# Agent attention with a gated convolution: query weights laid out in overlapping groups of four columns, 22 agents copied from rows four apart, and one buffer of transposed rows per batch

## The chip, the core and the metric

The kernel runs on one core of a Trainium2 chip. The metric is device time in microseconds (us), the median of several executions. The core has five engines with a queue each: PE (matmuls; its weight loads are shown as PEld), DVE (vector), ACT (scalar), POOL (GpSimd) and SP, which here only issues DMA transfers. A queue is worked off in order: an instruction that waits holds up all that stand behind it. Engines wait for each other through semaphores.

## The reference, cut to what matters

```
B, N, C = 4, 12800, 128          # 49 agents per batch
def sm(a, b):                    # softmax over the last axis
    s = (a @ b.T) / sqrt(C);  e = exp(s - max(s));  return e / (sum(e) + 1e-9)
agent_v = sm(agents, k) @ v      # 49 x 128 per batch
x       = sm(q, agents) @ agent_v            # N x 128
gate    = sigmoid(sum_k conv_w[k] * x[n - 4 + k])   # 5 taps, causal, zeros ahead of a batch
out     = (gate * (x @ w_val)) @ w_out
```

All inputs and the output are float32.

## The kernel before, in words

**Folding.** x itself is never made. Since x = W agent_v, with W the 49 softmax weights of each query, the five taps of the gate and the value projection are linear in W. For each batch `fold_weights` (lines 513 to 730) multiplies agent_v by the five tap weights and by w_val, so that the gate and the value of a query come straight from its weights W and those of the four queries ahead of it. The main loop is then matmuls over rows of W (one row an agent, one column a query).

**Three products for one.** The matmuls run in float16, and a float32 number is held as a high and a low part. For each agent three products are needed: high weight by high matrix, low weight by high matrix, high weight by low matrix. That is 147 rows; a matmul takes 128. The 128 rows of `pt` (lines 777 to 798) are 49 low parts (POOL, L794), 49 high parts (ACT, L779) and 30 of the high parts again (POOL, L784). The high parts of the 19 agents that are left lie in a second tile, `x2`, each five times, shifted by one query from tap to tap: 95 rows, so that one matmul serves all taps (L926 for the gate, L953 for the value). The matrices beside them, `wst`, are built row by row to match (lines 570 to 631) and transposed on PE (L659) into `stat`.

**Units, pairs, chunks.** A unit is 1280 queries (10 units a batch, 40 in all). `queries` (lines 733 to 798): scores on PE (L376), transposed by DVE (L386), maximum (L745), subtraction on POOL (L750), exp on ACT (L758), sums (L763 to L767) and scaling (L772) on DVE, then the three steps that fill `pt`. `transposes` (line 827) turns `pt` into rows of W: on PE for the first four units (L849), by a DMA transpose from SP's queue for the other 36 (L835). Two units make a pair (20 in all, 5 a batch), which has a buffer of 2560 columns, one of a ring of four tiles `x1s`. The last four columns of the pair before are needed ahead of a pair's first column: `halo` (lines 813 to 825) copies them on POOL (L819), or writes zeros (L816) at the head of a batch. `shifts` (lines 866 to 891) then issues two DMA copies from x1 into x2 (L884), 15 agents and 4 agents. `gates`, `values` and `project` (lines 898 to 1025) work on chunks of 512 queries, 25 a batch: five tap matmuls (L922) and the x2 matmul (L926) for the gate, tanh on ACT (L935); two matmuls for the value (L949, L953); their product h on DVE (L962), its high part hh on ACT (L968), its low part hl on POOL (L973); three matmuls for the output (L992 to L994), scaled on ACT (L1006), and stored from SP (L1021).

**Keys and values.** Each batch also has ten units of keys (L376 again, copied by ACT at L402, maximum at L411) and ten of values (exp at L471, transposed at L386, matmuls at L480). Units of q, k and v are loaded by SP (L369) into a ring of 11 buffers.

**What sets the order.** PE's order is written out by hand (`order`, lines 1088 to 1114). The orders of ACT, DVE, POOL and SP come from a list scheduler (`Plan`, lines 68 to 173): each step carries an engine, an estimated cost in us, what it reads and writes and, for a transfer, the time on the wire; of the steps that are ready the one with the longest tail of work behind it goes first. When the estimates change, or steps fall away, the order of these four queues may change everywhere.

Of the kernel before, what the change touches and what calls it, by code (L numbers as in the profile page):

```python
# [32 lines left out]
THREES = 15  # L33
NDUP = 2 * THREES
X2R = 19
X2CUTS = ((0, THREES, 3, 0.5), (THREES, X2R, 1, 0.3))

# [4 lines left out]
NX = 4  # L42
# [134 lines left out]
def tile_agent_attention_gated_conv(  # L177
# [39 lines left out]
    qw = ring(NPT, [P, NBLK, A], F32, "qw")  # L217
# [3 lines left out]
    x1s = ring(NX, [P, PAD + SEG], F16, "x1_")  # L221
# [39 lines left out]
    tiny = const.tile([P, NBLK], F32, name="tiny")  # L261
    nc.scalar.dma_start(out=ag_sb, in_=agT)
# [6 lines left out]
    nc.vector.memset(x1s[0][:, 0:PAD], 0.0)  # L269
    for t in wst_sb:  # L270
        nc.gpsimd.memset(t[:, TAPS + 1 :, :], 0.0)
# [232 lines left out]
    avT = const.tile([P, A], F32, name="avT")  # L504
    mx = const.tile([P, 2], F32, name="mx")
    gw = const.tile([P, TAPS, A], F32, name="gw")
    gs = const.tile([P, TAPS, A], F32, name="gs")
# [5 lines left out]
    def fold_weights(b):  # L513
# [19 lines left out]
        def normalise():  # L533
            dve.tensor_scalar_add(den, pt[:, 0:A], 1e-9)
            dve.reciprocal(out=den, in_=den)
            dve.tensor_tensor(out=avT, in0=pt[:, AP_ : AP_ + A], in1=den, op=ALU.mult)
# [5 lines left out]
                out=gw, in0=avT.unsqueeze(1).to_broadcast([P, TAPS, A]),  # L542
                in1=conv_sb.unsqueeze(2).to_broadcast([P, TAPS, A]), op=ALU.mult,
# [4 lines left out]
        def gate_scale():  # L548
# [16 lines left out]
                out=pv[:, 0:A], lhsT=wval_sb, rhs=avT, start=True, stop=True  # L565
# [4 lines left out]
        x2g = wst[:, TAPS + 1, 0 : TAPS * X2R].rearrange("p (r k) -> p k r", k=TAPS)  # L570
        x2v = wst[:, TAPS + 2, 0 : TAPS * X2R].rearrange("p (r k) -> p k r", k=TAPS)
        ghi = wst[:, 0:TAPS, 0:A]
        vhi = wst[:, TAPS, 0:A]

        def threes(x):

            if len(x.shape) == 2:
                return x[:, 0 : 3 * THREES].rearrange("p (i r) -> p i r", r=3)
            return x[:, :, 0 : 3 * THREES].rearrange("p k (i r) -> p k i r", r=3)

        def rest(out, full, s, hi):
            dve.scalar_tensor_tensor(
                out=out, in0=full, scalar=rs[:, s : s + 1], in1=hi,
                op0=ALU.mult, op1=ALU.subtract,
            )

        def val_weights():
# [9 lines left out]
            dve.tensor_scalar_mul(vhi, pv[:, 0:A], rs[:, 1:2])  # L597
# [8 lines left out]
        def gate_weights():  # L606
            dve.tensor_scalar_mul(ghi, gw, rs[:, 0:1])
# [579 lines left out]
```

## Time and profile before

| | |
|---|---|
| three runs | 425.52, 428.47, 429.88 us; median 428.47 |
| profiled execution, first to last instruction (span) | 423.6 us |
| profiled execution, its own time | not on record beside its span |
| PE, DVE, ACT, POOL busy | 403.9, 293.3, 301.5, 228.2 us |
| mean granted clock of PE | 0.985 |
| moved by DMA | 127.62 MB, 301 GB/s on average |

How to read it: busy time is the time in which an engine had at least one instruction under way; loads of weights (PEld) overlap matmuls. A wait is put down to what ended last ahead of it. In a table of stretches, each engine's busy us stand in order PE, PEld, DVE, ACT, POOL, followed by the granted clock of PE, the DMA engines' mean busy share (packets overlap, so that it can pass 1) and GB/s. In a timeline, each row has start, duration, engine, line, operation, written tile and read tiles, and in brackets the idle time ahead of it with its releaser; "x" stands for x1, x1s and x2 alike, since buffer numbers are left out.

### The profile page before, as it was taken

To read this page: it belongs to the slowest core of one execution; us is meant where nothing else is said; L and a number is where in the kernel's file an instruction comes from. 1 tells how busy PE (TensorE), PEld (TensorE's weight loads), DVE (VectorE), ACT (ScalarE), POOL (GpSimd) and SP (SyncE) were. 2 spreads that over 40 slices of the span, in tenths; PEclk is the share of its full clock that TensorE was granted. 3 is DMA by queue.
4 is the path that set the end of the run, shared out by engine and by line. 5 is a ranking of instruction groups with operands and counts; after the bars stand their busy time and mean duration, and the time that the engine had idled before them with its cause. 6 is when DMAs were issued, how large, how long until landed. Compare 5 with 4: busy or idle time off the path is not lost.

```text
span 423.6 us, 10042 instructions
## 1 busy us (share of the span) xinstructions
PE 403.9 (95%) x3907; PEld 197.0 (47%) x3907; DVE 293.3 (69%) x562; ACT 301.5 (71%) x521; POOL 228.2 (54%) x263
## 2 busy tenths in 40 slices
PE   4979999999999999999999899999999989999995
PEld 1358434346555443446555343335555534344443
DVE  3757899867875978667795575767765678676231
ACT  1564568779966777678876486778876567788776
POOL 1002557654657565554566355574366277877553
PEclk9969999999999999999999899999999999999998
DMA  8999999999999999999999999999999977755733
GB/s 320 420 417 411 370 367 353 301 295 310 412 293 283 346 317 362 304 278 356 351 379 324 271 299 370 314 332 302 296 393 322 239 196 161 199 163 176 205 121 124
DMA packets 75129, 127.62 MB, mean 301 GB/s; under 512 B 50466, under 2 KB 50850, under 8 KB 75084
## 3 DMA queue, kind: packets, MB, share of 16 engines
q1 hardware_dynamic: 74940, 126.87, 96.9%
q8 instruction: 30, 0.49, 0.5%
q10 hardware_dynamic: 144, 0.13, 0.2%
q14 instruction: 15, 0.12, 0.1%
HBM read 79.25 MB, written 26.21 MB: 249 GB/s over the span
## 4 chain that ended last, share of the span: by engine, by line
PE 78%; DMA 9%; DVE 8%; ACT 1%; POOL 1%; issue 1%; SPq 0%; POOLq 0%; DVEq 0%; ACTq 0%
PE gate L922 23%; PE sc L376 17%; PE av L480 10%; PE val L949 5%; PE out L992 5%; PE val L953 5%; PE gate L926 5%; PE out L993 4%; DMA ld<-kT 4%; PE out L994 4%; DMA x<-pt 3%; DMA x<-x 2%; DVE h L962 1%; DVE qw L772 1%; DVE qsm L763 1%
## 5 line engine op out<-in xcount | busy, mean ns | idle before, releaser
L973 POOL TENSOR_TENSOR hl<-h,hh 128x512 f16<-128x512 f32 (+1 forms) x101 | 116.9, 1158 | 96.1 <-ACT hh L968 96.0
L922 PE MATMUL gate<-x,stat 128*128 128x512 f16 (+1 forms) x500 | 125.2, 380 | 0.2 <-ACT th L935 0.2
L962 DVE SCALAR_TENSOR_TENSOR h<-th,val 128x512 f32<-128x512 f32 x100 | 67.8, 678 | 66.8 <-PE out L993 26.2
L376 PE MATMUL sc<-ld,ag_sb 128*32 128x320 f32 x1280 | 101.5, 447 | 7.6 <-DMA ld<-kT 7.0
L935 ACT ACTIVATE th<-gate,unscale 128x512 f32<-128x512 f32 x100 | 68.3, 683 | 33.3 <-PE gate L926 31.7
L1006 ACT ACTIVATE ob<-out,oscale 128x512 f32<-128x512 f32 x98 | 67.3, 687 | 21.3 <-PE out L994 20.1
L922 PEld LDWEIGHTS <-stat 128*128 128x128 f16 x505 | 46.3, 97 | 63.7 <-issue 14.8
L968 ACT CAST hh<-h 128x512 f16<-128x512 f32 (+1 forms) x101 | 61.5, 609 | 17.2 <-DVE h L962 16.4
L750 POOL TENSOR_TENSOR qw<-sT,qmx 128x490 f32<-128x490 f32 x40 | 41.4, 1035 | 47.6 <-DVE qmx L745 47.5
L376 PEld LDWEIGHTS sc<-ld,ag_sb 128*32 128x32 f32 x1280 | 36.7, 111 | 59.4 <-issue 25.7
L480 PE MATMUL av<-ld,eT 128*32 128x129 f32 (+1 forms) x1400 | 50.7, 279 | 1.0 <-DVE eT L386 1.0
L480 PEld LDWEIGHTS av<-ld,eT 128*32 128x32 f32 (+1 forms) x1400 | 47.1, 117 | 7.5 <-issue 2.5
L794 POOL TENSOR_TENSOR pt<-qw,pt 128x490 f16<-128x490 f32 x40 | 44.8, 1120 | 3.1 <-ACT pt L779 2.9
L471 ACT ACTIVATE e<-ks,kbias 128x320 f32<-128x320 f32 x80 | 39.3, 554 | 5.4 <-DVE eT L386 3.3
L386 DVE STREAM_TRANSPOSE sT<-sc 128x640 f32<-128x640 f32 x40 | 33.6, 839 | 13.4 <-PE sc L376 12.7
L402 ACT COPY ks<-sc 128x640 f32<-128x640 f32 x40 | 27.7, 691 | 21.2 <-PE sc L376 19.1
L386 DVE STREAM_TRANSPOSE eT<-e 128x640 f32<-128x640 f32 x40 | 33.5, 842 | 9.8 <-ACT e L471 5.2
L926 PE MATMUL gate<-x,stat 95*128 95x512 f16 x100 | 38.3, 383 | 1.5 <-DMA x<-x 1.5
L949 PE MATMUL val<-x,stat 128*128 128x512 f16 x100 | 38.2, 382 | 0.8 <-DVE h L962 0.6
L953 PE MATMUL val<-x,stat 95*128 95x512 f16 x100 | 38.1, 381 | 0.0
L994 PE MATMUL out<-hl,wo 128*128 128x512 f16 x98 | 37.0, 378 | 1.1 <-POOL hl L973 1.1
L992 PE MATMUL out<-hh,wo 128*128 128x512 f16 x98 | 37.3, 381 | 0.1
(130 smaller groups left out, 389.4 us busy)
## 6 DMA issues: line engine op xcount, KB each, us to landing
ld<-kT SPq DMA_DIRECT2D x40, 640.0 KB
ld<-qT SPq DMA_DIRECT2D x40, 640.0 KB
ld<-vP SPq DMA_DIRECT2D x39, 645.0 KB
outT<-ob SPq DMA_DIRECT2D x48, 512.0 KB
x<-x SPq DMA_DIRECT2D x18, 375.0 KB
x<-x SPq DMA_DIRECT2D x18, 100.0 KB
outT<-ob SPq DMA_DIRECT2D x3, 256.0 KB
x<-x SPq DMA_DIRECT2D x4, 187.5 KB
```

What stands on the lines that cost most here:

```text
L376: nc.tensor.matmul(out=out[g * BLK : (g + 1) * BLK, j, 0:GT], lhsT=ag_sb[:, b, j * BLK : (j + 1) * BLK], rhs=src[:, g * GT : (g + 1) * GT] ...
L386: nc.vector.transpose(out=out.rearrange("p n (j i) -> p j n i", j=2), in_=in_.rearrange("p j (n i) -> p j n i", i=BLK),)
L480: nc.tensor.matmul(out=av[o + j : o + j + cols, 0 : C + 1], lhsT=et[:, n, j : j + cols], rhs=vt[:, n, :], start=(u == 0 and n < 2), stop=( ...
L922: nc.tensor.matmul(out=pg, lhsT=stat[:, k, :], rhs=x1[:, c : c + w], start=(k == 0), stop=False,)
L926: nc.tensor.matmul(out=pg, lhsT=stat[0 : TAPS * X2R, TAPS + 1, :], rhs=x2[0 : TAPS * X2R, o2 : o2 + w], start=False, stop=True,)
L935: lambda: nc.scalar.activation(out=th, in_=pg, func=AF.Tanh, scale=unscale[:, 0:1]),
L949: nc.tensor.matmul(out=pv, lhsT=stat[:, TAPS, :], rhs=x1s[(b * NCH + n0 // CH) // 5 % NX][:, PAD + o2 : PAD + o2 + w], start=True, stop=False,
L953: nc.tensor.matmul(out=pv, lhsT=stat[0 : TAPS * X2R, TAPS + 2, :], rhs=x2[0 : TAPS * X2R, o2 : o2 + w], start=False, stop=True,)
L962: lambda: nc.vector.scalar_tensor_tensor(out=h, in0=th, scalar=1.0, in1=pv, op0=ALU.add, op1=ALU.mult),
L968: "act", 0.16 + 0.42 * scale, lambda: nc.scalar.copy(out=hh, in_=h),
L973: lambda: nc.gpsimd.tensor_tensor(out=hl, in0=h, in1=hh, op=ALU.subtract),
L1006: lambda: nc.scalar.activation(out=ob[:, o : o + w], in_=po, func=AF.Copy, scale=oscale),
```

## The change

- **Layout of `pt`** (rows of W). Rows 32 to 99 now hold 17 groups of four: group i holds the high parts of agents 3i-1 to 3i+2, so that every third agent stands there twice. `qw` is 52 columns wide, with a zero column ahead of the 49 and two behind them, and is read in groups of four that start every three columns. ACT writes 680 elements a block row in place of 490. Low parts lie in rows 98 to 127 and 0 to 20 (two POOL subtractions, 300 and 210 elements, in place of one of 490); 11 more duplicates lie in rows 21 to 31 (110 elements in place of 300).
- **x2** holds 22 agents in place of 19: 16 from rows 34, 38, ..., 94 and 6 from rows 77, 81, ..., 97, in partitions 16 to 125. Its matmuls take all 128 partitions, of which the others are zero.
- **x1** is one tile with five pairs of a batch side by side behind 16 zero columns, in place of a ring of four. The columns ahead of a pair are the tail of the pair before it, so `halo` is gone.
- **Weights.** `wst` follows the new layout: the high parts are written into the groups, ACT copies the high parts into the rows that meet low weights in two steps (`lows`) in place of one, and there are four remainders (`rests`) for gate and value. `gw`, `gs` and `avT` are 51 wide; `gs` borrows an output buffer.
- **Setup.** POOL clears `wst` as a whole, the three x2 tiles and the four qw tiles.
- Estimates for the planner: ACT 0.58 to 0.75 us, POOL 0.44 to 0.3 and 1.09 to 1.3, x2 copies 0.5 + 0.3 to 0.5 + 0.2 a unit.

The diff, cut to its core:

```diff
@@ -30,16 +30,34 @@
...
-THREES = 15
-NDUP = 2 * THREES
-X2R = 19
-X2CUTS = ((0, THREES, 3, 0.5), (THREES, X2R, 1, 0.3))
+AW = 52
+HI = 32
+FOURS = 17
+LOWS = ((HI + 4 * FOURS - 2, 0, 10), (0, 10, FOURS - 10))
+TWICE = 11
+AGAIN = HI - TWICE
+X2R = 22
+X2O = 16
+X2CUTS = ((0, 16, HI + 2, 0.5), (16, X2R, HI + 1 + 4 * TWICE, 0.2))
+def fours(x):
+    return x[:, :, HI : HI + 4 * FOURS].rearrange("p n (i r) -> p n i r", r=4)
+def threes(x, first, n, width):
+    ap = [tuple(d) for d in x.ap]
+    return bass.AP(x.tensor, x.offset + first, ap[:2] + [(3, n), (1, width)])
...
-NX = 4
+NX = 5
@@ -214,11 +232,11 @@
...
-    qw = ring(NPT, [P, NBLK, A], F32, "qw")
+    qw = ring(NPT, [P, NBLK, AW], F32, "qw")
...
-    x1s = ring(NX, [P, PAD + SEG], F16, "x1_")
+    x1 = const.tile([P, PAD + NX * SEG], F16, name="x1")
@@ -259,6 +277,7 @@
...
+    avT = const.tile([P, AW - 1], F32, name="avT")
@@ -266,9 +285,12 @@
...
-    nc.vector.memset(x1s[0][:, 0:PAD], 0.0)
+    nc.vector.memset(avT, 0.0)
+    nc.vector.memset(x1[:, 0:PAD], 0.0)
...
-        nc.gpsimd.memset(t[:, TAPS + 1 :, :], 0.0)
+        nc.gpsimd.memset(t, 0.0)
+    for t in x2s + qw:
+        nc.gpsimd.memset(t, 0.0)
@@ -501,10 +523,9 @@
...
-    avT = const.tile([P, A], F32, name="avT")
...
-    gw = const.tile([P, TAPS, A], F32, name="gw")
-    gs = const.tile([P, TAPS, A], F32, name="gs")
+    gw = const.tile([P, TAPS, AW - 1], F32, name="gw")
+    gs = obs[3][:, 0 : TAPS * (AW - 1)].rearrange("p (k a) -> p k a", k=TAPS)
@@ -533,14 +554,14 @@
         def normalise():
...
-            dve.tensor_tensor(out=avT, in0=pt[:, AP_ : AP_ + A], in1=den, op=ALU.mult)
+            dve.tensor_tensor(out=avT[:, 0:A], in0=pt[:, AP_ : AP_ + A], in1=den, op=ALU.mult)
         add("dve", 0.8, normalise, [at_t], ["avT"])
         add(
...
-                out=gw, in0=avT.unsqueeze(1).to_broadcast([P, TAPS, A]),
-                in1=conv_sb.unsqueeze(2).to_broadcast([P, TAPS, A]), op=ALU.mult,
+                out=gw, in0=avT.unsqueeze(1).to_broadcast([P, TAPS, AW - 1]),
+                in1=conv_sb.unsqueeze(2).to_broadcast([P, TAPS, AW - 1]), op=ALU.mult,
@@ -562,27 +583,43 @@
         add(
...
-                out=pv[:, 0:A], lhsT=wval_sb, rhs=avT, start=True, stop=True
+                out=pv[:, 0 : AW - 1], lhsT=wval_sb, rhs=avT, start=True, stop=True
...
-        x2g = wst[:, TAPS + 1, 0 : TAPS * X2R].rearrange("p (r k) -> p k r", k=TAPS)
-        x2v = wst[:, TAPS + 2, 0 : TAPS * X2R].rearrange("p (r k) -> p k r", k=TAPS)
-        ghi = wst[:, 0:TAPS, 0:A]
-        vhi = wst[:, TAPS, 0:A]
-        def threes(x):
-            if len(x.shape) == 2:
-                return x[:, 0 : 3 * THREES].rearrange("p (i r) -> p i r", r=3)
-            return x[:, :, 0 : 3 * THREES].rearrange("p k (i r) -> p k i r", r=3)
-        def rest(out, full, s, hi):
-            dve.scalar_tensor_tensor(
-                out=out, in0=full, scalar=rs[:, s : s + 1], in1=hi,
-                op0=ALU.mult, op1=ALU.subtract,
-            )
+        x2g = wst[:, TAPS + 1, X2O : X2O + TAPS * X2R].rearrange("p (r k) -> p k r", k=TAPS)
+        x2v = wst[:, TAPS + 2, X2O : X2O + TAPS * X2R].rearrange("p (r k) -> p k r", k=TAPS)
+        x2v = x2v[:, HALO : HALO + 1, :]
+        wg, wv = wst[:, 0:TAPS, :], wst[:, TAPS : TAPS + 1, :]
+        ghi, vhi = fours(wg), fours(wv)
+        pv3 = pv[:, 0 : AW - 1].unsqueeze(1)
+        def rests(full, hi, out, x2_, less):
+            n = X2R - 16
+            less(out[:, :, HI + 4 : HI + 4 * FOURS : 4], full[:, :, 2:A:3], hi[:, :, 0:16, 3])
+            less(out[:, :, AGAIN:HI], full[:, :, 0 : 3 * TWICE : 3], hi[:, :, 0:TWICE, 1])
+            less(x2_[:, :, 0:16], full[:, :, 1:A:3], hi[:, :, 0:16, 2])
+            less(x2_[:, :, 16:], full[:, :, 3 * TWICE : A : 3], hi[:, :, TWICE : TWICE + n, 1])
+        def lows(out, hi):
+            for to, i0, n in LOWS[::-1]:
+                nc.scalar.copy(
+                    out=out[:, :, to : to + 3 * n].rearrange("p k (i r) -> p k i r", r=3),
+                    in_=hi[:, :, i0 : i0 + n, 1:4],
+                )
+        def rest(s):
+            def less(out, full, hi):
+                dve.scalar_tensor_tensor(
+                    out=out, in0=full, scalar=rs[:, s : s + 1], in1=hi,
+                    op0=ALU.mult, op1=ALU.subtract,
+                )
+            return less
         def val_weights():
@@ -594,17 +631,11 @@
...
-            dve.tensor_scalar_mul(vhi, pv[:, 0:A], rs[:, 1:2])
-            pv3, hi3 = threes(pv[:, 0:A]), threes(vhi)
-            rest(
-                wst[:, TAPS, 2 * A :].rearrange("p (i r) -> p i r", r=2),
-                pv3[:, :, 0:2], 1, hi3[:, :, 0:2],
-            )
-            rest(x2v[:, HALO, 0:THREES], pv3[:, :, 2], 1, hi3[:, :, 2])
-            rest(x2v[:, HALO, THREES:], pv[:, 3 * THREES : A], 1, vhi[:, 3 * THREES :])
+            dve.tensor_scalar_mul(vhi[:, :, :, 1:4], threes(pv3, 0, FOURS, 3), rs[:, 1:2])
+            rests(pv3, vhi, wv, x2v, rest(1))
         def gate_weights():
-            dve.tensor_scalar_mul(ghi, gw, rs[:, 0:1])
+            dve.tensor_scalar_mul(ghi[:, :, :, 1:4], threes(gw, 0, FOURS, 3), rs[:, 0:1])
         def gate_scaled():
@@ -615,37 +646,27 @@
             def less(out, full, hi):
...
-            gs3, hi3 = threes(gs), threes(ghi)
-            twos = wst[:, 0:TAPS, 2 * A :].rearrange("p k (i r) -> p k i r", r=2)
-            for r in range(2):
-                less(twos[:, :, :, r], gs3[:, :, :, r], hi3[:, :, :, r])
-            less(x2g[:, :, 0:THREES], gs3[:, :, :, 2], hi3[:, :, :, 2])
-            less(x2g[:, :, THREES:], gs[:, :, 3 * THREES :], ghi[:, :, 3 * THREES :])
+            rests(gs, ghi, wg, x2g, less)
         def gate_rest():
-            gw3, hi3 = threes(gw), threes(ghi)
-            twos = wst[:, 0:TAPS, 2 * A :].rearrange("p k (i r) -> p k i r", r=2)
-            for r in range(2):
-                rest(twos[:, :, :, r], gw3[:, :, :, r], 0, hi3[:, :, :, r])
-            rest(x2g[:, :, 0:THREES], gw3[:, :, :, 2], 0, hi3[:, :, :, 2])
-            rest(x2g[:, :, THREES:], gw[:, :, 3 * THREES :], 0, ghi[:, :, 3 * THREES :])
+            rests(gw, ghi, wg, x2g, rest(0))
...
         if b == 0:
             add("pool", 0.4, gate_scaled, ["gw", "rsg"], ["gs"])
-            add("act", 0.4, lambda: nc.scalar.copy(out=ghi, in_=gs), ["gs"], [(*w_, "g")])
+            add("act", 0.4, lambda: nc.scalar.copy(out=ghi[:, :, :, 1:4], in_=threes(gs, 0, FOURS, 3)), ["gs"], [(*w_, "g")])
             add("pool", 1.0, gate_rest_pool, ["gs", (*w_, "g")], [(*w_, "r")])
...
             add("dve", 0.4, gate_weights, ["gw", "rsg"], [(*w_, "g")])
         add("dve", 1.2, val_weights, [at_v], [(*w_, "v"), "mxv"])
         add(
...
-            lambda: nc.scalar.copy(out=wst[:, 0:TAPS, A : 2 * A], in_=ghi),
+            lambda: lows(wg, ghi),
...
         add(
-            "act", 0.22, lambda: nc.scalar.copy(out=wst[:, TAPS, A : 2 * A], in_=vhi),
+            "act", 0.4, lambda: lows(wv, vhi),
@@ -735,7 +756,8 @@
...
-        sT, d, e, w, r, sm = sts[x], qw[g % NPT], qw[g % NPT], qw[g % NPT], qr[x], qsm[x]
+        sT, wide, r, sm = sts[x], qw[g % NPT], qr[x], qsm[x]
+        d = e = w = wide[:, :, 1 : 1 + A]
...
         add("pe", 1.07, lambda: score_matmuls(b, ld[i], ps), [("ld", i), ("ld2", i)], [at], key="sc")
@@ -775,54 +797,47 @@
...
-        add(
-            "act", 0.58, lambda: nc.scalar.copy(out=pt[:, :, A : 2 * A], in_=w),
+        hi = fours(pt)
+        add(
+            "act", 0.75, lambda: nc.scalar.copy(out=hi, in_=threes(wide, 0, FOURS, 4)),
...
         add(
-            "pool", 0.44,
+            "pool", 0.3,
...
-                out=pt[:, :, 2 * A :].rearrange("p n (i r) -> p n i r", r=2),
-                in0=w[:, :, 0 : 3 * THREES].rearrange("p n (i r) -> p n i r", r=3)[:, :, :, 0:2],
-                scalar1=1.0, scalar2=0.0,
-                op0=ALU.mult, op1=ALU.add,
+                out=pt[:, :, AGAIN:HI], in0=w[:, :, 0 : 3 * TWICE : 3],
+                scalar1=1.0, scalar2=0.0, op0=ALU.mult, op1=ALU.add,
...
-        add(
-            "pool", 1.09,
-            lambda: nc.gpsimd.tensor_tensor(
-                out=pt[:, :, 0:A], in0=w, in1=pt[:, :, A : 2 * A], op=ALU.subtract
-            ),
-            [("qw", g % NPT), (*p_, 0)], [(*p_, 1)],
-        )
+        def lower():
+            for to, i0, n in LOWS[::-1]:
+                nc.gpsimd.tensor_tensor(
+                    out=pt[:, :, to : to + 3 * n].rearrange("p n (i r) -> p n i r", r=3),
+                    in0=threes(wide, 1 + 3 * i0, n, 3), in1=hi[:, :, i0 : i0 + n, 1:4], op=ALU.subtract,
+                )
+        add("pool", 1.3, lower, [("qw", g % NPT), (*p_, 0)], [(*p_, 1)])
     def on_pe(b, u):
...
+    def pair_at(s):
+        return PAD + s % NX * SEG
     def unit_rows(g):
-        o = PAD + g % 2 * UNIT
-        return x1s[g // 2 % NX][:, o : o + UNIT]
+        o = pair_at(g // 2) + g % 2 * UNIT
+        return x1[:, o : o + UNIT]
     def row_keys(s, halves):
-        i = s % NX
-        return [(x, i, h) for h in halves for x in ("x1", "x1b")] + [("x1h", i)] * (0 in halves)
-    def halo(s):
-        to = x1s[s % NX][:, PAD - HALO : PAD]
-        if s * 2 % NU == 0:
-            fn = lambda: nc.gpsimd.memset(to, 0.0)
-            read = []
-        else:
-            fn = lambda: nc.gpsimd.tensor_copy(
-                out=to, in_=x1s[(s - 1) % NX][:, PAD + SEG - HALO : PAD + SEG]
-            )
-            read = [(x, (s - 1) % NX, 1) for x in ("x1", "x1b")]
-        read.append(("x2", (s - 1) % 3, UNIT, 0))
-        add("pool", 0.1, fn, read, [("x1h", s % NX)])
+        keys = [(x, s % NX, h) for h in halves for x in ("x1", "x1b")]
+        if 0 in halves and s % NX:
+            keys += [(x, s % NX - 1, 1) for x in ("x1", "x1b")]
+        return keys
     def transposes(b, u):
@@ -871,24 +886,21 @@
...
-        x2, x1 = x2s[s % 3], x1s[s % NX]
+        x2 = x2s[s % 3]
...
-        c = PAD - HALO + o
-        for r0, r1, every, us in X2CUTS:
-            first = A + (2 if every == 3 else 3 * THREES)
-            rows = x1[first : first + 1 + (r1 - r0 - 1) * every : every, c : c + 1]
+        c = pair_at(s) - HALO + o
+        for r0, r1, first, us in X2CUTS:
+            rows = x1[first : first + 1 + (r1 - r0 - 1) * 4 : 4, c : c + 1]
...
             add(
...
-                    out=x2[r0 * TAPS : r1 * TAPS, o : o + n * UNIT],
+                    out=x2[X2O + r0 * TAPS : X2O + r1 * TAPS, o : o + n * UNIT],
...
-        if g % 2 and (g + 1) // 2 < B * NU // 2:
-            halo((g + 1) // 2)
@@ -909,7 +921,8 @@
...
-        x2, x1 = x2s[segs_[0] % 3], x1s[segs_[0] % NX]
+        x2 = x2s[segs_[0] % 3]
+        o1 = pair_at(segs_[0])
@@ -918,14 +931,14 @@
         def matmuls():
...
-                c = PAD - HALO + o2 + k
+                c = o1 - HALO + o2 + k
...
-                out=pg, lhsT=stat[0 : TAPS * X2R, TAPS + 1, :],
-                rhs=x2[0 : TAPS * X2R, o2 : o2 + w], start=False, stop=True,
+                out=pg, lhsT=stat[:, TAPS + 1, :], rhs=x2[:, o2 : o2 + w],
+                start=False, stop=True,
@@ -935,24 +948,24 @@
...
-        return stat, x2, o2, xs, x2k, st, th
+        return stat, x2, o1 + o2, o2, xs, x2k, st, th
...
     def values(t):
...
-        stat, x2, o2, xs, x2k, st, th = state.pop(t)
+        stat, x2, o1, o2, xs, x2k, st, th = state.pop(t)
...
         def matmuls():
...
-                out=pv, lhsT=stat[:, TAPS, :], rhs=x1s[(b * NCH + n0 // CH) // 5 % NX][:, PAD + o2 : PAD + o2 + w],
+                out=pv, lhsT=stat[:, TAPS, :], rhs=x1[:, o1 : o1 + w],
...
-                out=pv, lhsT=stat[0 : TAPS * X2R, TAPS + 2, :],
-                rhs=x2[0 : TAPS * X2R, o2 : o2 + w], start=False, stop=True,
+                out=pv, lhsT=stat[:, TAPS + 2, :], rhs=x2[:, o2 : o2 + w],
+                start=False, stop=True,
```

## The prediction

> **What bounds the kernel now.** First the page's head and its chain.
>
> ```profile
> span 423.6 us, 10042 instructions
> PE 403.9 (95%) x3907; PEld 197.0 (47%) x3907; DVE 293.3 (69%) x562; ACT 301.5 (71%) x521; POOL 228.2 (54%) x263
> DMA  8999999999999999999999999999999977755733
> PE 78%; DMA 9%; DVE 8%; ACT 1%; POOL 1%; issue 1%; SPq 0%; POOLq 0%; DVEq 0%; ACTq 0%
> ```
>
> PE is busy for all but 20 us, most of the chain is PE following PE, and until the last fifth the DMA engines are as full. PE work can't shrink here, so the waits of PE come next: line, releaser, us in all, times, longest.
>
> ```profile
> PE sc L376 <- DMA ld<-kT: 7.0, 4, 6.1
> PE gate L926 <- DMA x<-x: 1.5, 1, 1.5
> PE out L994 <- POOL hl L973: 1.1, 1, 1.1
> ```
>
> The first belongs to the first key load and stays. Two waits lie in the steady part, and both touch what is changed. The stretches around them (busy us of PE, PEld, DVE, ACT, POOL; granted clock; DMA share; GB/s):
>
> ```profile
> 230.00:240.00 10.00, 8.50 (x107) 4.72 (x100) 5.10 (x14) 3.67 (x7) 4.97 (x7) 0.85 1.14 290
> 330.00:340.00 10.00, 9.02 (x106) 4.66 (x95) 6.04 (x13) 4.32 (x8) 3.21 (x5) 1.00 1.10 226
> 340.00:350.00 10.00, 9.28 (x60) 4.46 (x60) 7.64 (x25) 7.26 (x14) 7.25 (x10) 1.00 0.80 193
> ```
>
> From 230 to 240 PE loses 1.50 us idle and then as much again to the clock (0.85 over 10 us, 1.5 us). From 330 to 350 it loses 0.98 + 0.72 = 1.70 us, at full clock. Nearly everything that an edit away from PE can win lies in these 4.7 us. On the timelines of PE and of SP's queue, the first loss is:
>
> ```profile
> 235.67 0.39 PE L926 MATMUL gate<-x,stat 95*128 95x512 f16 x1 [1.50 <-DMA x<-x]
> 236.89 2.24 PE L922 MATMUL gate<-x,stat 128*128 128x512 f16 x5
> ```
>
> ```profile
> 212.77 7.23 SPq L835 DMA_TRANSPOSE x<-pt  x1
> 220.10 0.53 SPq L369 DMA_DIRECT2D ld<-kT  x1
> 220.73 2.63 SPq L835 DMA_TRANSPOSE x<-pt  x1
> ...
> 228.28 1.65 SPq L884 DMA_DIRECT2D x<-x  x2
> ```
>
> SP sits 7.23 us in one transpose, so the next waits until 220.73; it has landed by 228.28, when the two x2 copies go out, and these land at 235.6, 7.35 us later. The gate comes 1.5 us too early for them. The second loss, on POOL:
>
> ```profile
> 331.70 1.09 POOL L794 TENSOR_TENSOR pt<-qw,pt 128x490 f16<-128x490 f32 x1 [0.18 <-ACT pt L779]
> 338.78 0.19 POOL L819 COPY x<-x 128x4 f16<-128x4 f16 x1 [5.99 <-DMA x<-pt]
> 338.93 2.27 POOL L973 TENSOR_TENSOR hl<-h,hh 128x512 f16<-128x512 f32 x2
> ```
>
> The halo copy (L819) stands 5.99 us at the head of POOL's queue for a transpose to land; two hl subtractions are queued behind it, and PE's 1.1 us at L994 is the wait for them.
>
> **The change part by part.**
>
> *Halo.* Gone are 16 copies (0.19 us) and 3 memsets (0.10), some 3.3 us of POOL, and their wait:
>
> ```profile
> POOL x L819 <- DMA x<-pt: 16.4, 5, 6.0
> ```
>
> Of these 16.4 us, PE felt 1.1. The transpose that the copy waited for is no faster without it; next in line then is pair 15's x2 copy, issued as that transpose lands and due at about 338.8 + 7.35 = 346.1, while its first gate (chunk 75) reads it only at:
>
> ```profile
> 352.79 0.38 PE L926 MATMUL gate<-x,stat 95*128 95x512 f16 x1
> ```
>
> So the 1.1 us is won: **-1.1** (bounds 0 and -1.7, all of that stretch).
>
> *Wider high copy, other low rows, fewer duplicates.* Rows per group (busy us, mean ns of one, idle before):
>
> ```profile
> L968 ACT CAST hh<-h 128x512 f16<-128x512 f32 x99 | 60.7, 614 | 17.1 <-DVE h L962 16.4
> L968 ACT CAST hh<-h 128x256 f16<-128x256 f32 x2 | 0.8, 400 | 0.1
> L779 ACT CAST pt<-qw 128x490 f16<-128x490 f32 x40 | 23.9, 600 | 10.7 <-DVE qw L772 10.7
> ```
>
> ```profile
> L973 POOL TENSOR_TENSOR hl<-h,hh 128x512 f16<-128x512 f32 x99 | 115.5, 1168 | 94.8 <-ACT hh L968 94.7
> L973 POOL TENSOR_TENSOR hl<-h,hh 128x256 f16<-128x256 f32 x2 | 1.3, 671 | 1.3 <-ACT hh L968 1.3
> L794 POOL TENSOR_TENSOR pt<-qw,pt 128x490 f16<-128x490 f32 x40 | 44.8, 1120 | 3.1 <-ACT pt L779 2.9
> L784 POOL TENSOR_SCALAR pt<-qw 128x300 f16<-128x300 f32 x40 | 18.2, 457 | 20.6 <-DVE qw L772 20.6
> L616 POOL TENSOR_TENSOR wst<-gs,wst 128x75 f16<-128x75 f32 x3 | 1.1, 403 | 0.5 <-ACT wst L637 0.5
> ```
>
> An ACT cast is (614-400)/256 = 0.84 ns an element and 186 ns: 490 gives 596 (row: 600), 680 give 754, +0.15 us a unit and 6.2 us over 40. POOL's subtraction is 1.94 ns and 174 ns: one of 490 becomes 300 and 210, 756 + 582 = 1338 ns, +0.22. The duplicate goes from 300 elements to 110; between a price by elements (168 ns) and none saved (457) I take -0.10. POOL: +0.12 x 40 - 3.3 = +1.5 us. No row has ACT reading overlapping groups of four; the nearest strided row, L616, takes 403 ns for 75 elements against 174 + 146 = 320 by the line above, 1.1 ns an element more, which on 680 would be +0.75 us a unit, 30 us of ACT. Below, a gain is excluded: more elements, the same operation. I take zero, since all groups but the borders lie next to each other. What covers this: ACT is idle 29% and POOL 46% of the span, and the 7.23 us in SP's queue, which outlast a unit that is ready 0.3 us later. Without that cover it is 0.3 us on a tight pair. **0** (0 to +1).
>
> [...]
>
> *x2: 22 agents on 110 rows instead of 19 on 95.* The issue table and the packets (KB each):
>
> ```profile
> x<-x SPq DMA_DIRECT2D x18, 375.0 KB
> x<-x SPq DMA_DIRECT2D x18, 100.0 KB
> ```
>
> ```profile
> DMA packets 75129, 127.62 MB, mean 301 GB/s; under 512 B 50466, under 2 KB 50850, under 8 KB 75084
> ```
>
> A pair's copies grow from 475 to 400 + 150 = 550 KB, +15.8%; 75 KB x 20 is 1.5 MB, at 301 GB/s 5.1 us of transfer. The loads are not late anywhere after the start (no wait of PE on them), so what counts is the landing of a pair's copies. Bounds: unchanged, if it is queueing behind other transfers, and +15.8% of 7.35 us = +1.16 us, if it goes by their own bytes; a gain is bounded by the 1.5 us that the gate waits. I take **0**, nearer to queueing: 475 KB at 301 GB/s are 1.6 of the 7.35 us.
>
> [...]
>
> *Zero rows and memsets.* The x2 matmuls go from 95 to 128 contraction rows:
>
> ```profile
> L922 PE MATMUL gate<-x,stat 128*128 128x512 f16 x495 | 124.5, 381 | 0.2 <-ACT th L935 0.2
> L926 PE MATMUL gate<-x,stat 95*128 95x512 f16 x99 | 38.0, 384 | 1.5 <-DMA x<-x 1.5
> ```
>
> 381 against 384 ns: **0**. POOL clears x2, qw and the whole of wst at the start:
>
> ```profile
> L271 POOL MEMSET wst<- 128x256 f16 x2 | 0.6, 312 | 0.0
> 35.26 1.02 POOL L750 TENSOR_TENSOR qw<-sT,qmx 128x490 f32<-128x490 f32 x1 [32.94 <-DVE qmx L745]
> ```
>
> At no more than 1.22 ns an element, 2 x 1024 + 3 x 2560 + 4 x 520 elements are at most 14 us, under POOL's 32.94 us of idleness: **0**; without it up to 14 us.
>
> *Folded weights.* The value split has four remainders for three, ACT two low copies for one. Only the first fold is on the chain:
>
> ```profile
> 44.33 0.53 DVE wst L582 x3
> ```
>
> One more of these is 0.18 to 0.25 us, and the longer ACT part lies beside DVE: **+0.3** (0 to +0.6).
>
> *Order.* The planner gets new costs and loses the halo steps, so the queues of ACT, POOL, DVE and SP are laid out anew; no row prices this. The two waits of 1.1 and 1.5 us show what an unlucky place costs, either way.
>
> Sum: -1.1 + 0.3 = -0.8, span 422.8. The profiled execution's own time isn't on record beside its span; the runs were 425.5 to 429.9, so it was at most 1.9 us outside the span if it was as quick as the quickest. Applied to the median of 428.47: **427.7 us**.
>
> **The rivals.**
>
> *Both losses vanish.* The x2 copies land 1.5 us earlier and no queue holds POOL: -3.0 -1.7 = -4.7, 423.8 us. For it: the halo is gone for certain, the 1.5 us of idleness were a near miss. Against it: more bytes, and the same 7.23 us transpose ahead of them. [...]
>
> *x2 lands later (slower).* If landing goes by bytes, it is 1.16 us later, and 0.37 more where the query weights are (ACT +0.15, POOL +0.22). Besides pair 9 above, pair 4 is tight: its copies go out at 127.74, due by 135.1, and its gate's x2 matmul runs at 135.69.
>
> ```profile
> 127.74 1.67 SPq L884 DMA_DIRECT2D x<-x  x2
> ```
>
> ```profile
> 135.69 0.38 PE L926 MATMUL gate<-x,stat 95*128 95x512 f16 x1
> ```
>
> 1.53 us later costs pair 9 1.53 and pair 4 0.9 us, and the clock as much again: +4.9, 433.4 us. It decides from 0.6 us of lateness on. For it: DMA share 1.0 to 1.14; against it: queueing, above.
>
> *The single x1 buffer serialises.* If its writes waited for every earlier read of it, a pair's transposes and copies (some 15 us, 220.7 to 235.6) would no longer lie beside gates: 18 pairs x 15 = +270 us, near 700. Against it: L784 and L779 write one pt tile, and L784 waits for DVE alone, so waits go by region.
>
> **How the numbers follow.** The forecast, in which the change is all but hidden, 0.55; both losses gone 0.25; late x2 0.17; serialised 0.03. The first is within 1%, about what a measurement of this kernel tells from no change, the second 1.1% faster, the last two slower. Range 422.3 to 433.5: the first three cases, with 1.5 us below the second for a second near miss saved.
>
> **What would show it.** Right: no L819 and no wait of POOL on x<-pt; L994's wait gone; L779 at 0.75 us, L794's pair near 1.34; x2 landing 7 to 8 us after issue behind the v loads; 2 to 5 us of PE idleness from 60 us on. Wrong: PE waits on x<-x at several pairs or none; the clock under 1.00 in any other stretch; L779 near 1.5 us; PE waiting for L994 again behind another POOL step.

## The result, and the profile after

The changed kernel takes 447.21 us (median of 5 runs, 444.89 to 450.28) against 428.47 us for the kernel before (5 runs, 425.52 to 431.14): ratio 1.0465, 95% interval 1.0411 to 1.0518. It is slower, and 13.7 us above the top of the predicted range. Of the runs behind the times below, one each of e3 (1437.51 us), e5, e10 and e12 was slow: it counts in the median that is given and is left out of the ratio.

The page's head for the changed kernel (its own time 444.89 us, 1.9 us outside the span; granted clock 0.976 on average, 0.985 before):

```profile
span 443.0 us, 10078 instructions
PE 406.3 (92%) x3907; PEld 195.9 (44%) x3907; DVE 300.2 (68%) x567; ACT 307.7 (69%) x529; POOL 241.1 (54%) x291
PEclk9989999999998999999999899999999689999999
DMA  8999999999997999969999899999989976654633
PE 55%; DMA 18%; DVE 15%; ACT 5%; issue 3%; POOL 3%; SPq 1%; POOLq 0%; DVEq 0%; ACTq 0%
```

PE does the same 3907 matmuls in a span that is 19.4 us longer. DMA has gone from 9% of the chain to 18%, while the DMA row, full before until the last fifth, now has gaps in the middle (a 7, a 6, two 8s). Transfers are late, yet the DMA engines stand idle more: so they are issued late. PE's waits (line, releaser, us in all, times, longest):

```profile
PE gate L939 <- DMA x<-x: 17.6, 7, 8.8
PE sc L398 <- DMA ld<-kT: 7.4, 7, 5.7
PE val L454 <- DVE m L447: 3.1, 1, 3.1
```

L939 is the gate's x2 matmul, L926 before, where it waited once for 1.5 us. Outside its busy time PE now stands for 36.7 us of the span (443.0 - 406.3), and for 19.7 before (423.6 - 403.9): 17.0 of the 19.4 us are idle time, and L939's 17.6 us in seven waits for 1.5 account for 16.1 of them. The other 2.4 us are busy time, with the same matmuls at a mean granted clock of 0.976 for 0.985. Three stretches show idle time and clock together (columns as in the prediction):

```profile
240.00:250.00 10.00, 5.48 (x24) 3.03 (x28) 3.73 (x11) 2.40 (x5) 2.00 (x3) 0.83 0.83 204
340.00:350.00 10.00, 2.10 (x27) 0.81 (x15) 2.04 (x6) 0.62 (x1) 1.44 (x2) 0.83 1.09 271
350.00:360.00 10.00, 9.15 (x42) 3.69 (x42) 3.77 (x10) 3.93 (x7) 2.86 (x4) 0.65 0.74 204
```

PE stands idle for 4.5 and 7.9 us, and in the 10 us after the second gap the granted clock is 0.65.

SP's queue, which issues the transfers, tells what is late. Its waits:

```profile
SPq L850 <- DMA x<-x: 61.9, 19, 7.6
SPq L898 <- DMA x<-pt: 39.1, 16, 4.4
SPq L850 <- POOL hl L986: 37.8, 16, 8.1
```

L850 is the DMA transpose into x1, L898 the x2 copy out of it. The second row is the order that the data demands: a copy waits for the transposes of its own pair. The first row is new: transposes wait for x2 copies, 61.9 us in 19 waits. On SP's timeline:

```profile
235.70 1.43 SPq L898 DMA_DIRECT2D x<-x  x2
237.23 0.40 SPq L391 DMA_DIRECT2D ld<-qT  x1
244.56 1.30 SPq L850 DMA_TRANSPOSE x<-pt  x1
245.91 0.77 SPq L391 DMA_DIRECT2D ld<-kT  x1
246.79 1.34 SPq L850 DMA_TRANSPOSE x<-pt  x1
...
251.99 1.43 SPq L898 DMA_DIRECT2D x<-x  x2
253.52 0.41 SPq L391 DMA_DIRECT2D ld<-kT  x1
261.71 1.31 SPq L850 DMA_TRANSPOSE x<-pt  x1
```

The copies go out at 235.70; the next transpose is not issued before they have landed, at 244.5; it must land in turn before the copies of 251.99, and the next transpose waits for these until 261.71. Copy, transpose, copy, each some 8 us, stand one behind the other where the prediction had them side by side, and loads and stores queue behind the waiting transpose. The chain of waits has the two kinds in a row:

```profile
227.47 8.21 DMA x<-pt
235.68 0.02 issue
235.70 0.60 SPq L898
236.31 0.05 issue
236.35 8.12 DMA x<-x
244.47 0.05 issue
244.52 0.61 PE gate L939
```

No data asks for this order. The copies read the columns of pair s, the transposes write those of pair s+1, elsewhere in x1. But the program holds the wait, as its instructions on SP's queue show (number, operation, semaphores waited for; semaphores 5 and 6 are those of the two copies above it):

```
61 DMA x2<-x1 80x1x2560 [waits DMAHW7,DMAHW5,DMAHW1]
62 DMA x2<-x1 30x1x2560 [waits DMAHW6]
64 DMA_TRANSPOSE x1<-pt2 [waits DMAHW5,DMAHW0,DMAHW6,Activation,Pool]
```

16 of the 36 DMA transposes carry such a wait for copies of the pair before (a write that waits for an earlier read, in short a write-after-read wait). The theory (A): the dependence tracking of the language takes the read of every fourth row of the one x1 tile and the write next to it for overlapping, and SP's queue, worked off in order, turns that into a serial chain. Its rivals: the new row layout with its larger x2 copies costs the time (B), or the new order of the four planned queues does (C).

### The profile page after: what moved, and what is told of

It reads as the page before. It is cut to its first block, busy times and chain, and to the rows that moved or that the text cites. A ratio compares the mean times of both kernels' runs of the same rounds, so it can differ in the third digit from the quotient of the medians.

```text
span 443.0 us, 10078 instructions
## 1 busy us (share of the span) xinstructions
PE 406.3 (92%) x3907; PEld 195.9 (44%) x3907; DVE 300.2 (68%) x567; ACT 307.7 (69%) x529; POOL 241.1 (54%) x291
## 4 chain that ended last, share of the span: by engine, by line
PE 55%; DMA 18%; DVE 15%; ACT 5%; issue 3%; POOL 3%; SPq 1%; POOLq 0%; DVEq 0%; ACTq 0%
PE gate L935 15%; PE sc L398 11%; DMA x<-pt 10%; DMA x<-x 7%; PE av L502 7%; PE val L962 4%; PE out L1005 3%; PE gate L939 3%; PE out L1006 3%; PE val L966 3%; PE out L1007 3%; DVE ob L318 2%; DVE h L975 2%; DVE kmx L433 2%; DVE qsm L785 2%
## 5 line engine op out<-in xcount | busy, mean ns | idle before, releaser
L981 ACT CAST hh<-h 128x512 f16<-128x512 f32 (+1 forms) x101 | 61.4, 608 | 16.1 <-DVE h L975 15.6
L816 POOL TENSOR_TENSOR pt<-qw,pt 128x210 f16<-128x210 f32 x80 | 55.0, 688 | 19.0 <-ACT pt L802 15.8
L939 PE MATMUL gate<-x,stat 128*128 128x512 f16 x100 | 38.3, 383 | 17.6 <-DMA x<-x 17.6
L502 PE MATMUL av<-ld,eT 128*32 128x129 f32 (+1 forms) x1400 | 48.5, 275 | 0.5 <-DVE eT L408 0.5
L502 PEld LDWEIGHTS av<-ld,eT 128*32 128x32 f32 (+1 forms) x1400 | 45.0, 114 | 7.3 <-issue 1.9
L962 PE MATMUL val<-x,stat 128*128 128x512 f16 x100 | 38.6, 386 | 0.7 <-DVE h L975 0.5
L966 PE MATMUL val<-x,stat 128*128 128x512 f16 x100 | 38.5, 385 | 0.0
L1005 PE MATMUL out<-hh,wo 128*128 128x512 f16 x98 | 38.0, 388 | 0.1
L1006 PE MATMUL out<-hh,wo 128*128 128x512 f16 x98 | 37.9, 387 | 0.0
```

Source lines behind the costliest of these rows:

```text
L502: nc.tensor.matmul(out=av[o + j : o + j + cols, 0 : C + 1], lhsT=et[:, n, j : j + cols], rhs=vt[:, n, :], start=(u == 0 and n < 2), stop=( ...
L816: nc.gpsimd.tensor_tensor(out=pt[:, :, to : to + 3 * n].rearrange("p n (i r) -> p n i r", r=3), in0=threes(wide, 1 + 3 * i0, n, 3), in1=hi ...
L962: nc.tensor.matmul(out=pv, lhsT=stat[:, TAPS, :], rhs=x1[:, o1 : o1 + w], start=True, stop=False,)
L966: nc.tensor.matmul(out=pv, lhsT=stat[:, TAPS + 2, :], rhs=x2[:, o2 : o2 + w], start=False, stop=True,)
L981: "act", 0.16 + 0.42 * scale, lambda: nc.scalar.copy(out=hh, in_=h),
```

## The experiments

The kernel before ran beside each group: 427.01 us with the first four, 426.64 with the next four, 426.74 with the last four. Ratios are to these, intervals 95%.

**e1, the layout alone.** The changed kernel with the ring of four tiles and the halo put back.

```diff
-NX = 5
+NX = 4
-    x1 = const.tile([P, PAD + NX * SEG], F16, name="x1")
+    x1s = ring(NX, [P, PAD + SEG], F16, "x1_")
...
+        if g % 2 and (g + 1) // 2 < B * NU // 2:
+            halo((g + 1) // 2)
```

> The change without the single buffer: the groups of four, 22 agents and 110 rows of x2, the memsets, but x1 as a ring of four tiles with the halo copies, as before. Theory A (one tile): with x1 as a single tile the next pair's transposes wait for the x2 copies of the pair before, and that wait alone makes the change slow; so this kernel is back within 1% of 428.5 us (424 to 433), and SP no longer waits at the transposes for x<-x (61.9 us in the changed kernel, 0 here). Theory B (the new layout: 15.8% more x2 bytes, a wider ACT copy, two POOL subtractions): this kernel stays slow, 442 to 450. Theory C (the queues were merely laid out anew, and unluckily): anywhere between, with PE's waits for x<-x at other pairs.

Measured 430.13 us, 1.0065 (1.0032 to 1.0099). SP's longest wait is the old one, for hl:

```profile
SPq L859 <- POOL hl L996: 57.1, 19, 6.6
```

So B carries 0.65%, not 4.65%.

**e2, the buffer alone.** The kernel before with one x1 tile of five pairs and no halo; rows, x2 and weights as before.

```diff
-NX = 4
+NX = 5
-    x1s = ring(NX, [P, PAD + SEG], F16, "x1_")
+    x1 = const.tile([P, PAD + NX * SEG], F16, name="x1")
```

> The kernel before with one part of the change: x1 as one tile of five pairs behind zero columns, no halo; the old layout with 19 agents from rows three apart. Theory A: slow like the change, 442 to 450 us, with SP waiting 40 to 60 us at the transposes for x<-x and PE 10 us or more for x<-x. Theory B: 426 to 429, a little quicker than before since the halo is gone. Theory C: between.

Measured 438.69 us, 1.0278 (1.0244 to 1.0311). The new wait is there without the new layout:

```profile
SPq L826 <- DMA x<-x: 56.1, 13, 6.4
```

In this program 15 of the 36 transposes carry it, all for the copy of 15 agents: of the two old copies only that one reads rows with gaps (every third). The time lies below theory A's 442 to 450, so one buffer alone doesn't give the whole loss.

**e3, neighbouring rows, one buffer.** As the last, but the duplicates are agents 0 to 29, so that x2 takes agents 30 to 48 from 19 rows next to each other. No transpose then waits for copies of the pair before, though the row is the 25632 bytes of e2.

```diff
-X2CUTS = ((0, THREES, 3, 0.5), (THREES, X2R, 1, 0.3))
+X2CUTS = ((0, 15, 0.5), (15, X2R, 0.3))
...
+            rows = x1[A + NDUP + r0 : A + NDUP + r1, c : c + 1]
```

> The single buffer of e2, but the 30 agents held twice are 0 to 29 and the 19 agents of x2 are 30 to 48, so that the copies read rows that lie next to each other instead of three apart; the transposes then carry no wait for the copies. Theory A: 424 to 430 us, since both the wait and the halo are gone. A rival, A' (any single tile is slow, whatever rows are read, or the reads from neighbouring rows land later): 440 or more, with PE waiting for x<-x and landings above 9 us.

Measured 448.3 us, 1.0477 (1.0423 to 1.0532). By theory A it should have lost the penalty. It lost the wait (SP's longest was again for hl, 56.7 us in 18), and PE waited for x<-x even longer:

```profile
PE gate L901 <- DMA x<-x: 22.8, 7, 11.2
```

A second cost had come in with the rows; e8 below takes it apart.

**e4, no halo.** The kernel before without its halo steps; the four columns ahead of each pair are zero. It leaves out the earlier taps of a pair's first four queries.

```diff
-    nc.vector.memset(x1s[0][:, 0:PAD], 0.0)
+    for t in x1s:
+        nc.vector.memset(t[:, 0:PAD], 0.0)
...
-        if g % 2 and (g + 1) // 2 < B * NU // 2:
-            halo((g + 1) // 2)
```

> The kernel before with the halo steps left out (the four columns ahead of each pair stay zero, so the first four queries of a pair inside a batch lack their earlier taps). The prediction's step: the halo held POOL for 16.4 us and PE felt 1.1 of it, so 1.1 us less than before, 427.4 us, 0.2 to 0.4% quicker, and the wait of L994 for hl is gone. Rival: the wait only moves to the next landing and the time is that of before within 0.1%; or the new order of the queues costs more than 1.1 us.

Measured 423.51 us, 0.9923 (0.9897 to 0.9949): 3.3 us, three times what was predicted. The stretches that the prediction quoted are now:

```profile
230.00:240.00 10.00, 8.64 (x120) 5.26 (x112) 6.02 (x16) 4.41 (x8) 4.78 (x6) 1.00 1.09 311
330.00:340.00 10.00, 9.51 (x81) 4.22 (x73) 5.77 (x16) 5.47 (x10) 5.31 (x6) 1.00 1.08 283
340.00:350.00 10.00, 10.00 (x68) 4.65 (x65) 8.89 (x27) 7.85 (x15) 6.65 (x8) 1.00 0.94 249
```

PE's wait for hl is gone, as expected. From 330 to 350 PE is busy 19.51 us for 18.30; from 230 to 240 it still waits, but at clock 1.00 for 0.85. These two stretches would make up the 2.7 us between the two spans (423.6 and 420.9), but the runs don't bear out the clock's part: over the runs of this group the granted clock is the same on average, 0.992 without the halo and 0.991 with it, and the times still lie 3.3 us apart. In the two profiles PE is idle equally long as well (20.1 and 19.7 us). What carries the gain beyond 1.1 us stays open.

**e5, the changed kernel with 16 columns more.** Sixteen columns that nothing uses at the end of x1: a row is 25664 bytes for 25632. Every instruction stands where it stood, on every engine; the waits of transposes for earlier copies are gone.

```diff
-    x1 = const.tile([P, PAD + NX * SEG], F16, name="x1")
+    x1 = const.tile([P, PAD + NX * SEG + 16], F16, name="x1")
```

> The changed kernel with one number altered: x1 has 16 more columns that nothing uses, so a row is 25664 bytes instead of 25632. Every instruction of every engine stands in the same order as in the changed kernel; but the transposes carry no wait for the x2 copies any more (16 of 36 did). Theory A (that wait alone is what made the change slow; the copies and transposes are disjoint, and the wait is an overcautious one made from the tile's row length): 424 to 430 us, near the 427.7 of the prediction, SP waiting for x<-x at the transposes no more. Theory B (layout, x2 bytes) and theory C (order): 444 to 449 as the changed kernel, since layout and order are the same.

Measured 427.9 us, 1.0017 (0.9987 to 1.0047). The same transpose in its program, and its page, PE's waits and SP's:

```
64 DMA_TRANSPOSE x1<-pt2 [waits DMAHW0,Activation,Pool]
```

```profile
span 425.0 us, 10081 instructions
DMA  8999999999999999999999999999999988653733
```

```profile
PE gate L939 <- DMA x<-x: 4.4, 3, 2.8
```

```profile
SPq L850 <- POOL hl L986: 61.4, 18, 7.3
...
SPq L850 <- DMA x<-x: 1.3, 1, 1.3
```

L850's 61.9 us for x<-x have become 1.3, PE's 17.6 have become 4.4, and the gaps in the DMA row are closed. (In the programs without the new wait, this one too, a few transposes still wait for a copy eight transfers back, whose semaphore they use again; these waits are not counted here.) SP's timeline has the transpose right behind the copies:

```profile
228.43 1.43 SPq L898 DMA_DIRECT2D x<-x  x2
229.96 0.40 SPq L391 DMA_DIRECT2D ld<-qT  x1
230.47 1.43 SPq L850 DMA_TRANSPOSE x<-pt  x1
```

C falls, since the order is the same; so does B, since all of layout and x2 is still there.

**e6, the buffer alone with 16 columns more.** The same edit to e2.

```diff
-    x1 = const.tile([P, PAD + NX * SEG], F16, name="x1")
+    x1 = const.tile([P, PAD + NX * SEG + 16], F16, name="x1")
```

> The single buffer of e2 (old layout, no halo, outputs complete) with 16 more unused columns in x1: the same order as e2 and no wait of the transposes for the copies. Theory A: about the kernel without halo, e4, 422 to 426 us, so quicker than the kernel before by 0.5 to 1%. Otherwise (something else about one tile is slow): 436 to 440 as e2.

Measured 422.27 us, 0.9896 (0.9855 to 0.9938), where 1.0278 was without the columns.

**e7, the waits without buffer or layout.** The counter-test: e4 (so the same taps are left out), its ring of four cut from one tile with rows of 20640 bytes. That brings the wait back to 15 transposes (11 by the expectation); the order of every queue is that of e4, and no step and no byte is added.

```diff
-    x1s = ring(NX, [P, PAD + SEG], F16, "x1_")
+    x1 = const.tile([P, NX * (PAD + SEG) + 16], F16, name="x1")
+    x1s = [x1[:, i * (PAD + SEG) : (i + 1) * (PAD + SEG)] for i in range(NX)]
```

> The kernel without halo of e4 (first four queries of a pair lack their earlier taps), its ring of four now cut out of one tile with a row length that brings the waits back: 11 of the 36 transposes wait for an x2 copy, the rest of the order is that of e4. Theory A: 435 to 440 us, as e2 stood to e4's 423.5. If the waits are harmless: 422 to 425.

Measured 442.15 us, 1.0346 (1.0284 to 1.0407), against 0.9923 without the waits:

```profile
SPq L837 <- DMA x<-x: 57.9, 14, 7.0
```

The time is somewhat above theory A's 435 to 440. The wait alone makes a kernel 4.3% slower (1.0346 against 0.9923); taken away alone, it makes one 4.3% quicker (1.0017 against 1.0465). That the wait costs the time is shown from both sides. A row length by itself does not: e3 has the row of 25632 bytes without the wait, and e8 below, which has neither that buffer nor the wait, is no quicker than e3.

**e8, neighbouring rows, ring and halo.** The kernel before, with x2 read from 19 neighbouring rows as in e3, but no single buffer.

```diff
-X2CUTS = ((0, THREES, 3, 0.5), (THREES, X2R, 1, 0.3))
+X2CUTS = ((0, 15, 0.5), (15, X2R, 0.3))
```

> The kernel before, ring and halo kept, with the 19 agents of x2 read from neighbouring rows (15 and 4 rows of step 1 in place of 15 of step 3 and 4 of step 1). e3 had no wait of the transposes and was still slow (448). If neighbouring rows are what lands late: 440 to 452 us here too, with landings of the x2 copies 2 us or more above 7.4, PE waiting 10 us or more for x<-x. If it was the single buffer: 425 to 430.

Measured 449.83 us, 1.0525 (1.0485 to 1.0565). This is the whole of e3's loss, with no new wait in the program. PE's wait, and one landing from the chain:

```profile
PE gate L911 <- DMA x<-x: 20.8, 6, 9.8
```

```profile
132.36 9.44 DMA x<-x
```

That is the longest landing in its chain; the three others are 7.7 to 7.8 us, for 7.34 in the kernel before, so most landings are not the 2 us later that were expected. What has grown shows in the page's row for SP's transfers (packets, MB, share of 16 engines' span), first before, then here:

```profile
q1 hardware_dynamic: 74940, 126.87, 96.9%
q1 hardware_dynamic: 74940, 126.87, 97.5%
```

The same packets and bytes took 410 us of each DMA engine before (0.969 x 423.6) and 441 us here (0.975 x 452.5). e3, with the same rows, has 434 us; the changed kernel, e1, e2, e4 to e7, e9 and e11 lie between 402 and 414 us. With neighbouring rows the packets themselves take longer; why, no view names.

**e9 and e10, the padded buffer again, and with the change's memsets.** The kernel of e6 measured again, and beside it the same with the changed kernel's larger memsets.

```diff
-        nc.gpsimd.memset(t[:, TAPS + 1 :, :], 0.0)
+        nc.gpsimd.memset(t, 0.0)
+    for t in x2s + qw:
+        nc.gpsimd.memset(t, 0.0)
```

> The kernel of e6 again (single buffer with 16 unused columns, old layout), as the base for the other runs of this call, where single per cents are split. Expected 421 to 424 us, 0.7 to 1.3% quicker than the kernel before.

> The kernel of e6 with the memsets of the change at the start (wst as a whole, x2, qw on POOL), nothing else of its layout. Theory M (the new layout's 1.3% over e6 comes from the start: DVE's int32 steps took 1.6 us each beside the memsets, and PE's first wait for the key maximum grew from 1.3 to 2.8 us): 1.5 us above e6 or more, 423.5 to 426. Theory Q (it comes from the query units, ACT +0.15 and POOL +0.25 us each): as e6 within 0.5 us. Theory X (x2 bytes): as e6.

Measured 422.86 us, 0.9918 (0.9883 to 0.9952), and 422.59 us, 0.9887 (0.9851 to 0.9922). The memsets cost nothing that shows. With e6 these are the quickest complete kernels of the study, level within their intervals: the one buffer with its padded row, in the old layout.

**e11, the padded change with 19 agents in x2.** e5 without three agents of the second copy: 400 + 75 KB a pair, the bytes of before. It leaves out those agents' product of high weight and low matrix.

```diff
-                rows = x1[first : first + 1 + (r1 - r0 - 1) * 4 : 4, c : c + 1]
+                rows = x1[first : first + 1 + (min(r1, 19) - r0 - 1) * 4 : 4, c : c + 1]
```

> The padded change of e5 with three of the six agents of the second x2 copy left out (19 agents and 95 rows are copied, as before the change; the rows of the other three stay zero, so their product with the low part of the matrices is missing). Theory X (15.8% more x2 bytes make the copies land later): 423 to 425.5 us, most of the way from e5 to e6. Theories M and Q: 426.5 to 428.5, as e5.

Measured 424.36 us, 0.9938 (0.9911 to 0.9964), against 1.0017 (0.9987 to 1.0047) with all 22. The two intervals lie just apart. Against e12 below, which has all 22 agents and was measured beside it (1.0001, 0.9974 to 1.0027), they do too: the 75 KB a pair cost 0.6 to 0.8%, 2.3 to 3.4 us. PE's wait for the copies falls from 4.4 us to:

```profile
PE gate L939 <- DMA x<-x: 1.4, 2, 0.9
```

But that wait differs as much between two profiles of one and the same kernel, e6 and e9:

```profile
PE gate L916 <- DMA x<-x: 3.3, 2, 2.6
PE gate L916 <- DMA x<-x: 0.2, 1, 0.2
```

So one profile of each does not show that the bytes act through this wait.

**e12, the padded change with lean memsets.** e5, with wst and x2 cleared in 32-bit words, and of qw only the border columns.

```diff
-    for t in x2s + qw:
-        nc.gpsimd.memset(t, 0.0)
+    for t in x2s:
+        nc.gpsimd.memset(t.bitcast(I32), 0)
+    for t in qw:
+        nc.gpsimd.memset(t[:, :, 0:1], 0.0)
+        nc.gpsimd.memset(t[:, :, 1 + A :], 0.0)
```

> The padded change of e5 with leaner memsets: x2 and wst cleared as int32 words (half the elements) and only the three border columns of qw; the outputs are complete. POOL is then done with them by about 8 us instead of 12. Theory M: 1 us or more below e5, 425 to 426.8. Theories Q and X: as e5, 427 to 428.5.

Measured 426.67 us, 1.0001 (0.9974 to 1.0027). PE's wait for the first maximum of the keys (L454, here L457) falls from 2.8 us to 1.3, and the time is the same within the intervals.

## Why the prediction was wrong, point by point

**The failed step** is the last rival, "The single x1 buffer serialises", which the forecast set aside. It named the right place and was given 0.03, on the argument that "L784 and L779 write one pt tile, and L784 waits for DVE alone, so waits go by region". Those two steps run on compute engines and write columns of a tile on all its partitions; from them it was concluded for a DMA that reads every fourth partition. There the tracking isn't exact: whether it sees an overlap depended on the length of a row. With copies of every third or fourth row, programs with rows of 25632 and 20640 bytes hold the wait and those with 25664 don't; the two lengths that held it are odd multiples of 32 bytes. The rule inside the tracking was not read, so this is a description. The rival's price was off as well: 15 us for each of 18 pairs, near 700 us, supposed that PE had nothing else to do. Only 16 transposes wait, and PE has other units' scores, keys and values ahead of it; the wait came to 19.3 us (447.21 against e5's 427.9). The prediction's own sign of being wrong came with it: PE waits for x<-x at several pairs, in seven waits.

**Halo:** -1.1, measured -3.3 (e4) and with the padded buffer -3.5 to -4.4 (e9 and e6). Only PE's visible wait at L994 was counted, with a bound of -1.7 for all of that stretch; the gain is twice the bound, and what carries the rest is open (e4).

**x2's bytes:** 0, measured +2.3 to +3.4 (e11). The prediction took queueing, not bytes, to set the landing, and priced the other case at +1.16 us a landing with two tight pairs, +4.9 us in all, with the later query weights. The measured cost is about half of that or more. The 0 was the author's estimate, from 475 KB at 301 GB/s being 1.6 of the 7.35 us; no row shows what sets a landing. The landings in the chains are not later with the bytes as far as they go (8.11, 6.48 and 5.35 us in e5 with 550 KB a pair, 8.80 and 7.14 in e11 with 475 KB), but the time did move, so the bytes were not free. By which path they cost is not shown.

**Copies and duplicates** came out as costed:

```profile
L816 POOL TENSOR_TENSOR pt<-qw,pt 128x300 f16<-128x300 f32 x40 | 30.3, 757 | 3.1
L802 ACT CAST pt<-qw 128x680 f16<-128x680 f32 x40 | 30.2, 755 | 10.2 <-DVE qw L794 10.0
L816 POOL TENSOR_TENSOR pt<-qw,pt 128x210 f16<-128x210 f32 x40 | 24.7, 618 | 15.8 <-ACT pt L802 15.8
L807 POOL TENSOR_SCALAR pt<-qw 128x110 f16<-128x110 f32 x40 | 13.3, 332 | 28.8 <-DVE qw L794 28.8
```

755 ns for ACT's copy (754 predicted), 757 + 618 = 1375 for POOL's pair (1338), 332 for the duplicate (357). Overlapping groups of four cost ACT nothing extra. With the 174 ns of the subtraction taken off (an estimate: the duplicate is another operation), its 110 elements took (332 - 174) / 110 = 1.4 ns each and the old 300 took 0.94. That is half as much again for an element, with a read that steps over 12 bytes where the old one took two neighbours of every three. The prediction put a saving of 100 ns into its sum; 125 ns were saved.

**Zero rows and memsets:** 0 and 0. The x2 matmul of 128 rows takes 384 ns, as before, and the memsets' cost is inside the intervals.

**Folded weights** (+0.3) and **order** (not priced) have no run of their own; with the wider copies they are in what remains between e11 and e9 (0.9938 and 0.9918), which is inside the intervals.

**The sum.** Without the false wait the change stands at 427.9 us (e5), where 427.7 was predicted. That is luck and no support for the sum: a halo three times too small and bytes counted as nothing cancel. One buffer and layout cost more together (4.65%) than apart (0.65% and 2.8%). Of this, the layout costs 1.0 to 1.2% on the padded buffer (e5 against e9 and e6) for 0.65% on the ring, and the wait 4.5% (e5 to the changed kernel) for 3.6 to 3.9% in the old layout (e9 and e6 to e2). Both differences are close to the width of the intervals. That each waiting transpose then waits for two copies and not for one would explain the second, but was not tested.

## What to carry to other kernels

When several buffers are merged into one tile, look in the program, before any reasoning about overlap, at which semaphores each transfer waits for: a write-after-read wait between regions that don't touch is visible there, and a queue that is worked off in order passes it on to all that stands behind it (here 61.9 us of waits on SP's queue became 17.6 us of waits on PE). Test a suspected wait from both sides with an edit that changes nothing else, here 16 unused columns. A prediction that lands on the number of a mended kernel is not confirmed by that; each term has to be measured by itself.

## What the runs showed of the hardware

**Source rows of a copy.** Reading 19 neighbouring rows in place of rows three apart made the kernel 5.25% slower (e8), at the same packets and bytes, which took 441 us of each DMA engine for 410. What in the choice of rows makes the packets slower, no row shows.

**DVE beside POOL's memsets.** The first steps of both in the changed kernel:

```profile
3.54 6.58 POOL L293 MEMSET x<- 128x2560 f16 x3
4.00 8.36 DVE L318 TENSOR_SCALAR ob<-ob 128x261 int32<-128x261 int32 x2 [2.35 <-DMA ob<-moe]
10.05 1.95 POOL L293 MEMSET qw<- 128x520 f32 x4
```

In the kernel before, such a step takes:

```profile
L296 DVE TENSOR_SCALAR ob<-ob 128x261 int32<-128x261 int32 x6 | 1.7, 294 | 2.9 <-DMA ob<-moe 2.8
```

Two of them took 8.36 us, from 4.00 to 12.36, until POOL's memsets ended at 12.0. In the kernel before, where POOL's memset of wst ended at 2.32 us, the first two took 0.50 us, from 4.42; in the changed kernel the next one, at 12.86 us, took 0.30. In the chains of e5 and e11, with the memsets of the changed kernel, the first two take 8.07 and 7.97 us; the chain of e12, which has less to clear, holds no such step. So these two DVE steps were slow while POOL's memsets ran; by what they are held up is not shown. The prediction counted the memsets as hidden because POOL was idle, and did not ask what runs beside them. PE felt it at L454, where it waited 3.1 us for the first maximum and not the 1.3 of the kernel before and of e12; but the first transposes of the folded weights reached PE at 44.32 us, and at 45.03 in the kernel before, so the loss was made up by then, and the time shows none (e10, e12).
